# Softmax memory attention with two expert layers: clamps of the first weight conversions on GpSimd, first memory-times-weight products emitted earlier

## The chip, the cores and the metric

The kernel runs on one core of a Trainium2 chip. The time is that of one execution on the device, in microseconds (us). The engines are TensorE (PE; its weight loads are PEld), VectorE (DVE), ScalarE (ACT), GpSimd (POOL) and SyncE (SP), whose queue issues all DMAs. Each engine works through its instructions in the order in which the program gives them.

## The reference

For each of 8 x 8 heads (576 tokens, width 64, 32 memory slots):

```python
a = exp(phi - max(phi, tokens));  a = a / (sum(a, tokens) + 1e-9)
k_m = einsum('bhsm,bhsd->bhmd', a, k);  v_m = einsum('bhsm,bhsd->bhmd', a, v)
scores = q @ k_m.T / 8
attn = softmax(scores, memory slots)          # the kernel's p
x = attn @ v_m                                # [4608 tokens, 512]
```

Then two layers on the 4608 x 512 tokens, each with weights 512 x 2048 and 2048 x 512: `h = x @ w_in; x = (h - tanh(h)) @ w_out`, then `h = x @ w_in; out = elu(h) @ w_out`. The weights arrive as float64.

## The kernel before

Matrix products in the layers are done on pairs of a high and a low part (`hi`, `lo = a - hi`). In layer 1 the kernel does not form `attn @ v_m` first: it multiplies `v_m` with `w_in` (the `vw` products, lines 317 to 347), and then `vw` with p (`h_unit`, line 357, tile `h_ps`).

**Conversions.** `convert` (lines 40 to 64) turns 512 columns of float64 words into float32 with integer operations: the absolute value of the high word on ScalarE (line 48), a clamp of it on VectorE (line 50), a shift with a mask (line 51), and two more VectorE operations that add sign and low bits (lines 54, 57). The intermediate `cv_m` lies in PSUM, in a pool of one buffer. For the first four pages of `w_in` the last operation writes the weight itself (`whole`); otherwise it writes `cv_a` in SBUF (two buffers), ScalarE rounds it to `hi` (line 62) and GpSimd takes `lo` (line 64). A page is two conversions. The first 16 conversions are pages 0 to 3 of layer 1's `w_in` and `w_out`.

**Attention units.** The heads are worked off in 16 units of four heads (`unit`, from line 113). A unit reduces phi (`cmax`, line 123), transposes the maxima, spreads them with a matmul (`bmax`, line 136), subtracts (`a`, line 142), takes exponentials, forms k_m and v_m (`km`, line 157), transposes q (`pq`, line 182), forms scores (`sc`, line 202), transposes them on VectorE (line 204), and does the softmax: maximum and subtraction (lines 207, 208), exponential (line 210, ScalarE), sum, reciprocal and product (lines 212 to 215), transpose (line 218), `hi` and `lo` of p (lines 222, 223). Units 0 and 1 run these on VectorE; in later units `eng` is GpSimd for the operations written with `eng`. Units 0 and 1 send their p by DMA into the first blocks' tiles (line 230) as well as to DRAM (line 231). The phi tile has one buffer: the next unit's phi is loaded when `a` has been formed.

**The order of work.** The program's order is written by generators that are stepped in rounds: each `yield` ends a unit's or a conversion's step, `units.round()` and `cv.round()` step all that are alive. The prologue steps both until unit 1 is written out, and the two first `vw` pages come after that. Then 64 blocks of two `h_unit` calls follow, with conversions and units stepped between them; in block 1 a loop steps conversions and units together until the pages that it needs are converted. The set `converted` says that a conversion's instructions have been written into the program.

```python
        while 1 not in p_done:
            ...
            units.round()
            ...
        for pg in range(2):
            need("i", pg)
            m1.vw_whole(vm[0], wi[pg], pg, 0, 0)
```

Of the kernel before, what the change touches and what calls it, by code (L numbers as in the profile page):

```python
# [8 lines left out]
F32 = mybir.dt.float32  # L9
F32R = mybir.dt.float32r  # L10
I32 = mybir.dt.int32
U32 = mybir.dt.uint32
ACTF = mybir.ActivationFunctionType
ALU = mybir.AluOpType
# [4 lines left out]
B, H, S, D, M = 8, 8, 576, 64, 32  # L19
# [16 lines left out]
def r32(ap):  # L36
    return ap.bitcast(F32)


def convert(nc, pool, psum, raw, dst, whole=False):  # L40

    words = raw.bitcast(U32)
    w_lo, w_hi = words[:, 0::2], words[:, 1::2]
    lo_lim = 2.0 ** -15
    hi_lim = float.fromhex("0x1.fffffep+16")
    m = psum.tile(list(w_hi.shape), F32, tag="c", name="cv_m")
    mu = m.bitcast(U32)
    nc.scalar.activation(m, w_hi.bitcast(F32), ACTF.Abs)
    yield
    nc.vector.tensor_scalar(m, m, hi_lim, lo_lim, op0=ALU.min, op1=ALU.max)  # L50
    nc.vector.tensor_scalar(mu, mu, 3, 0x3FFFFFFF, op0=ALU.logical_shift_left, op1=ALU.bitwise_and)
    yield
    a = pool.tile(list(w_hi.shape), F32, tag="a", name="cv_a")
    nc.vector.scalar_tensor_tensor(mu, w_hi, 0xC0000000, mu, op0=ALU.bitwise_and, op1=ALU.bitwise_or)
    if whole:
        a = dst()
    nc.vector.scalar_tensor_tensor(a.bitcast(U32), w_lo, 29, mu, op0=ALU.logical_shift_right, op1=ALU.bitwise_or)
    if whole:
        return
    yield  # L60
    hi, lo = dst()
    nc.scalar.activation(hi, a, ACTF.Copy)
    yield
    nc.gpsimd.tensor_tensor(lo, a, r32(hi), op=ALU.subtract)  # L64


class Attention:
# [44 lines left out]
    def unit(self, u, nxt, eng, first_p=None):  # L112

        nc, wk, sm = self.nc, self.wk, self.sm
        b, g = divmod(u, 2)
        ident = self.ident
        kv, a, kT = self.kv, self.a, self.kT
# [5 lines left out]
        nc.vector.tensor_reduce(cmax, ph.rearrange("p h c m -> p h m c"), axis=AX.X, op=ALU.max)  # L123
        yield
        spaced = u >= 2
        mT = ps_tile([128, 96], "mT")
        nc.tensor.transpose(mT, cmax.rearrange("p h m -> p (h m)"), ident[:96, :96])
        nmax = sm.tile([128, 1], F32, tag="nmax", name="nmax")
# [8 lines left out]
        if spaced:  # L137
# [5 lines left out]
                          op=ALU.subtract)  # L143
# [31 lines left out]
        s = self.sc_p.tile([128, 18, M], F32, tag="s", name="s")  # L175
        for pr in range(2):
# [11 lines left out]
            if pr == 0:  # L188
# [6 lines left out]
                dst = self.vm_dst(b, g)  # L195
# [9 lines left out]
            yield  # L205
        smax = sm.tile([128, 18, 1], F32, tag="smax", name="smax")
        nc.vector.tensor_reduce(smax, s, axis=AX.X, op=ALU.max)
        nc.vector.tensor_tensor(s, s, smax.to_broadcast([128, 18, M]), op=ALU.subtract)
        yield
        nc.scalar.activation(s, s, ACTF.Exp, scale=1.0 / D ** 0.5)  # L210
        yield
        nc.vector.tensor_reduce(smax, s, axis=AX.X, op=ALU.add)
        nc.vector.tensor_scalar(smax, smax, GUARD, None, op0=ALU.add)
        nc.vector.reciprocal(smax, smax)
        eng.tensor_tensor(s, s, smax.to_broadcast([128, 18, M]), op=ALU.mult)
        yield
        pT = wk.tile([128, S], F32, tag="pT", name="pT")
        nc.vector.transpose(pT, s.rearrange("p j m -> p (j m)"))
# [1 line left out]
        phl = wk.tile([128, 2, 2, NB], F32R, tag="phl", name="phl")  # L220
        pTv = pT.rearrange("p (r s) -> p r s", r=2)
        nc.scalar.activation(phl[:, :, 0], pTv, ACTF.Copy)
        eng.tensor_tensor(phl[:, :, 1], pTv, r32(phl[:, :, 0]), op=ALU.subtract)
        yield
        if spaced:
            yield
# [304 lines left out]
def moe_kernel(tc, q, k, v, phi, w1, w2, w3, w4, out):  # L531
    nc = tc.nc
    with ExitStack() as top, tc.manual_schedule():
# [11 lines left out]
        m1 = Moe1(tc, l1a, const, p_dram, x2_dram)  # L545
# [3 lines left out]
        cv_p = new(l1b, "cv", 2, side="right")  # L549
# [3 lines left out]
        cv_ps = new(top, "ps_c", 1, space=PSUM)  # L553

        vm, vms = {}, {}
# [8 lines left out]
        wi, wo = {}, {}  # L564
        part = lambda t, h, c: t[:, h].rearrange("p a f -> p (a f)")[:, 512 * c:512 * c + 512]
        converted = set()

        def need(kind, pg, with_units=False):
            while not all((1, kind, pg, c) in converted for c in range(2)):
                cv.round()  # L570
                if with_units:
                    units.round()

        def conv(layer, kind, pg, c, lead=2):

            w = {("i", 1): w1, ("o", 1): w2, ("i", 2): w3, ("o", 2): w4}[kind, layer]
            raw = raw_p.tile([128, 512], mybir.dt.int64, tag="raw", name="raw")
            if kind == "i":
                src = w.rearrange("(k p) f -> p k f", p=128)[:, 2 * c:2 * c + 2, 256 * pg:256 * pg + 256]
                nc.sync.dma_start(out=raw.rearrange("p (a f) -> p a f", a=2), in_=src)  # L580
            else:
                r0 = 256 * pg + 128 * c
                nc.sync.dma_start(out=raw, in_=w[r0:r0 + 128, :])
            for k in range(lead + 1):
                yield k == lead
            staged, whole = [], (layer, kind) == (1, "i") and pg < 4

            def dst():
                if layer == 1:
                    ws = wi if kind == "i" else wo  # L590
                    if c == 0:
                        pool = wt_p[pg // 2 % (2 if kind == "i" else NSW)]
                        shape = [128, 2, 4, 256] if kind == "i" else [128, 2, 2, 512]
                        ws[pg] = pool.tile(shape, F32 if whole else F32R, tag=f"w{kind}{pg % 2}", name="w1")
                    if whole:
                        return part(ws[pg], 0, c)
                    return part(ws[pg], 0, c), part(ws[pg], 1, c)
                staged.append(wst_p[0].tile([128, 2, 512], F32R, tag="wst", name="wst"))
                return staged[-1][:, 0], staged[-1][:, 1]

            yield from convert(nc, cv_p, cv_ps, raw, dst, whole)
            converted.add((layer, kind, pg, c))
            if layer == 2:
                yield
                nc.sync.dma_start(out=w_dram[kind][pg, :, :, 512 * c:512 * c + 512], in_=r32(staged[-1]))

        conv_pair = lambda layer, kind, pg: [conv(layer, kind, pg, c) for c in range(2)]
        conv_l1 = lambda kind, *pgs: [g for pg in pgs for g in conv_pair(1, kind, pg)]
        conv_l2 = [g for pg in range(NPG) for kind in "io" for g in conv_pair(2, kind, pg)]
# [8 lines left out]
        for what in "phi", "kv", "q0", "q1":  # L618
            at0.load(0, what)
            at1.load(1, what)  # L620
        cv_first = [conv(1, "i", k // 2, k % 2, 0) for k in range(3)]
        cv = Staged([conv(1, "i", 1, 1)] + conv_l1("o", 0, 1), 2)
        cv.wait = 5
        for k, g in enumerate(cv_first):
# [3 lines left out]
        def unit(u):  # L628
            if u == 0:
                yield from at0.unit(u, 2 * B, nc.vector, first_p)  # L630
            else:
                yield from at1.unit(u, u + 1, nc.vector if u < 2 else nc.gpsimd, first_p if u == 1 else None)
# [2 lines left out]
        units = Staged()  # L635
        for u in range(2 * B):
            units.at((0, 1, 7, 13, 19, 25, 32, 39, 45, 52, 58, 65, 78, 85, 92, 99)[u], unit(u))
        while 1 not in p_done:
            if units.rounds >= 7:
                cv.half()  # L640
            units.round()
            if units.rounds >= 7:
                cv.round()
        pro.close()
        m1.ps_h = new(ps_h_ctx, "ps_h", 2, space=PSUM)
        at1.ps = misc
# [10 lines left out]
            nc.scalar.activation(vms[bp][:, 0], vm[bp], ACTF.Copy)  # L657
            nc.gpsimd.tensor_tensor(vms[bp][:, 1], vm[bp], r32(vms[bp][:, 0]), op=ALU.subtract)

        for pg in range(2):  # L660
            need("i", pg)
            m1.vw_whole(vm[0], wi[pg], pg, 0, 0)

# [6 lines left out]
        xq, pend, late = deque(), [], []  # L670
# [94 lines left out]
        for bi, (ss, bp, sub, j) in enumerate(blocks):  # L765
# [48 lines left out]
            for i in range(2):  # L814
                pg = 2 * sw + i
# [107 lines left out]
```

## Time and profile before

| what | us |
|---|---|
| median of 3 runs (1705.76 to 1710.95) | 1709.38 |
| the profiled execution, its own time | 1713.89 |
| its span, first to last instruction | 1712.1 |
| TensorE busy in the span | 1613.9 |
| first product of p with `vw` (`h_ps`, line 357) starts | 65.55 |

A row of a timeline gives the start and the duration of an instruction, or of several that follow each other, and in brackets the idle time of its engine ahead of it and what ended that. A row of waits sums the idle time of an engine ahead of a line by what ended it. TensorE's clock has two levels in the records, 1.2 and 2.4 GHz, given as 0.5 and 1.0.

### The profile page before, as it was taken

What the parts mean: (1) busy time and instruction counts of PE and PEld (TensorE: products, weight loads), DVE (VectorE), ACT (ScalarE), POOL (GpSimd) and SP (SyncE); (2) the same over time, 40 slices, a digit from 0 to 9 for tenths busy, and PEclk for the clock granted to TensorE, in tenths of its full rate; (3) what the DMA queues carried; (4) which work ended last, traced back from release to release, by engine and by line L of the source; (5) the groups of instructions that cost most, each with busy time, mean ns of one, the idle gap of its engine ahead of it and who ended that gap; (6) DMA issues with size and microseconds to landing.
All of it is one profiled execution on the core that took longest, in us unless ns stands there. A gap on an engine that the chain in (4) does not pass through costs nothing.

```text
span 1712.1 us, 26572 instructions
## 1 busy us (share of the span) xinstructions
PE 1613.9 (94%) x9884; PEld 1394.7 (81%) x9884; DVE 1187.0 (69%) x1730; ACT 931.0 (54%) x1677; POOL 757.2 (44%) x540
## 2 busy tenths in 40 slices
PE   5578999999989999999989999999999999999998
PEld 3346888787888999999989988888888888888886
DVE  4776767677989999999865655556555655565654
ACT  2455767677778888889853333333333333333332
POOL 1145655566666776767742222222222222222222
PEclk8668999999999999999999999999999999999999
DMA  8756566566565556666579321212121212121000
GB/s 194 213 172 179 176 188 198 182 201 226 192 212 176 170 193 219 220 214 215 182 238 360 103 62 48 74 49 63 49 74 42 70 50 74 50 65 59 25 14 25
DMA packets 140921, 236.09 MB, mean 138 GB/s; under 512 B 8184, under 2 KB 102392, under 8 KB 138744
## 3 DMA queue, kind: packets, MB, share of 16 engines
q1 hardware_dynamic: 140792, 234.39, 42.9%
q8 instruction: 78, 1.28, 0.3%
q14 instruction: 51, 0.42, 0.1%
HBM read 158.73 MB, written 74.45 MB: 136 GB/s over the span
## 4 chain that ended last, share of the span: by engine, by line
PE 65%; DVE 4%; DMA 4%; ACT 2%; issue 2%; POOL 1%; DVEq 0%; ACTq 0%; SPq 0%; POOLq 0%
PE h_ps L466 23%; PE o_ps L508 23%; PE x_ps L405 11%; PE h_ps L357 6%; PE vw_ps L328 1%; DMA p<-p_dram 1%; DMA xr<-x_dram 1%; DMA x_dram<-x 1%; DMA raw<-in_moe_w_in_dram 1%; DVE s L385 1%; DVE vw L333 1%; DVE h_ps L384 1%; ACT t L368 0%; DVE s L386 0%; POOL g L393 0%
## 5 line engine op out<-in xcount | busy, mean ns | idle before, releaser
L405 PE MATMUL x_ps<-g,w 128*128 128x288 f32 x3072 | 442.5, 297 | 11.8 <-POOL w L64 4.7
L492 POOL TENSOR_TENSOR e<-hm,e 128x512 fp32r<-128x512 f32 x144 | 187.1, 1299 | 576.9 <-ACT e L491 529.2
L405 PEld LDWEIGHTS x_ps<-g,w 128*128 128x128 f32 x3072 | 418.6, 189 | 25.6 <-ACT x L412 6.5
L466 PE MATMUL h_ps<-x,wi 128*128 128x512 f32 (+1 forms) x1920 | 424.6, 371 | 0.0
L508 PE MATMUL o_ps<-wo,e 128*128 128x512 f32 x1728 | 422.8, 393 | 0.7 <-POOL e L492 0.7
L466 PEld LDWEIGHTS h_ps<-x,wi 128*128 128x128 f32 x1920 | 336.1, 188 | 68.0
L508 PEld LDWEIGHTS o_ps<-wo,e 128*128 128x128 f32 x1728 | 323.4, 188 | 75.3 <-POOL e L492 1.1
L477 ACT ACTIVATE t_ps<-hm 128x512 f32<-128x512 f32 x144 | 86.7, 602 | 505.7 <-DVE hm L476 505.7
L375 POOL TENSOR_TENSOR v<-t,u 128x576 f32<-128x576 f32 x128 | 183.6, 1434 | 177.9 <-ACT u L369 161.1
L357 PE MATMUL h_ps<-p,vw 128*128 128x288 f32 x1536 | 240.2, 307 | 12.6 <-DVE s L386 6.6
L357 PEld LDWEIGHTS h_ps<-p,vw 128*128 128x128 f32 x1536 | 219.2, 196 | 24.5 <-issue 20.5
L483 DVE SCALAR_TENSOR_TENSOR hm<-hm,t_ps 128x512 f32<-128x512 f32 x144 | 99.1, 688 | 200.3 <-ACT hm L478 200.3
L393 POOL TENSOR_TENSOR g<-s,g 128x576 fp32r<-128x576 f32 x128 | 199.0, 1555 | 78.8 <-ACT g L392 71.5
L476 DVE TENSOR_SCALAR hm<-h_ps 128x512 f32<-128x512 f32 x144 | 99.6, 692 | 129.9 <-PE h_ps L466 129.2
L385 DVE SCALAR_TENSOR_TENSOR s<-s,v 128x576 f32<-128x576 f32 x128 | 137.3, 1073 | 7.3 <-POOL v L375 7.2
L368 ACT ACTIVATE t<-h_ps 128x576 f32<-128x576 f32 x128 | 83.3, 651 | 91.1 <-PE h_ps L357 38.8
L386 DVE COPY_PREDICATED s<-big,h_ps 128x576 f32<-128x576 uint32 x128 | 106.6, 833 | 12.8 <-ACT x L412 0.5
L370 ACT ACTIVATE s<-u,bias 128x576 f32<-128x576 f32 x128 | 99.5, 778 | 25.1 <-POOL g L393 15.5
L484 DVE SCALAR_TENSOR_TENSOR hm<-hm,t_ps 128x512 f32<-128x512 f32 x144 | 99.0, 688 | 5.0
L485 DVE TENSOR_TENSOR hm<-hm,h_ps 128x512 f32<-128x512 f32 x144 | 98.9, 687 | 5.0
L384 DVE TENSOR_TENSOR h_ps<-h_ps,t 128x576 f32<-128x576 f32 x128 | 96.6, 755 | 2.8 <-ACT u L369 2.7
L478 ACT ACTIVATE hm<-hm 128x512 f32<-128x512 f32 x144 | 91.0, 632 | 13.1
(88 smaller groups left out, 1681.2 us busy)
## 6 DMA issues: line engine op xcount, KB each, us to landing
x_dram<-x SPq DMA_DIRECT2D x128, 288.0 KB
xr<-x_dram SPq DMA_DIRECT2D x72, 512.0 KB
p<-p_dram SPq DMA_DIRECT2D x62, 576.0 KB
raw<-in_moe_w_in_dram SPq DMA_DIRECT2D x32, 512.0 KB
raw<-in_moe_w_out_dram SPq DMA_DIRECT2D x32, 512.0 KB
w_dram<-wst SPq DMA_DIRECT2D x32, 512.0 KB
kv<-in_k_dram SPq DMA_DIRECT2D x16, 576.0 KB
kv<-in_v_dram SPq DMA_DIRECT2D x16, 576.0 KB
```

What stands on the lines that cost most here:

```text
L357: nc.tensor.matmul(ps[:, j, :NB], lhsT=vw[a][:, kc, 128 * j:128 * j + 128], rhs=p[:, kc, b, :], start=(k == 0), stop=(k == 5))
L370: nc.scalar.activation(s, u, ACTF.Square, bias=bias[:, 0:1], scale=G_S)
L375: nc.gpsimd.tensor_tensor(v, t, u, op=ALU.mult)
L384: nc.vector.tensor_tensor(d, d, t, op=ALU.subtract)
L385: nc.vector.scalar_tensor_tensor(s, s, G_B, v, op0=ALU.add, op1=ALU.mult)
L386: nc.vector.copy_predicated(s, big.bitcast(U32), d)
L393: nc.gpsimd.tensor_tensor(g[:, 1], s, r32(g[:, 0]), op=ALU.subtract)
L405: nc.tensor.matmul(ps, lhsT=wo[pg][:, a, j, 128 * dm:128 * dm + 128], rhs=g[:, b, j, :], start=(k == 0), stop=(k == 11))
L466: nc.tensor.matmul(out, lhsT=w3[:, a, kc, 128 * j:128 * j + 128], rhs=x[:, b, kc, :], start=(i == 0), stop=(i == 11))
L476: nc.vector.tensor_scalar(hm, w[0], 0.0, None, op0=ALU.min)
L492: nc.gpsimd.tensor_tensor(e[:, 1], hm, r32(e[:, 0]), op=ALU.subtract)
L508: nc.tensor.matmul(acc, lhsT=e[:, a, jj, 128 * tg:128 * tg + 128], rhs=w4[:, b, j, :], start=(k == 0 and jj == 0 and i == 0), stop=(k == l ...
```

## The change

For the first 16 conversions ScalarE writes the absolute value to `cv_a` in SBUF, GpSimd clamps it there, and VectorE's first operation is the shift, from SBUF to `cv_m`. Both are written in the step of the absolute value, so a conversion has one step less. In unit 0 the subtraction of the maximum, the product with the reciprocal and the `lo` of p go to GpSimd (`beside`, `late`). The two first `vw` pages are written in the prologue, each as soon as its two conversions and `v_m` of units 0 and 1 are written.

```diff
-def convert(nc, pool, psum, raw, dst, whole=False):
+def convert(nc, pool, psum, raw, dst, whole=False, apart=False):
...
+    if apart:
+        a = pool.tile(list(w_hi.shape), F32, tag="a", name="cv_a")
+        nc.scalar.activation(a, w_hi.bitcast(F32), ACTF.Abs)
+        nc.gpsimd.tensor_scalar(a, a, hi_lim, lo_lim, op0=ALU.min, op1=ALU.max)
+        yield
+        m = psum.tile(list(w_hi.shape), F32, tag="c", name="cv_m")
+        mu = m.bitcast(U32)
+        nc.vector.tensor_scalar(mu, a.bitcast(U32), 3, 0x3FFFFFFF, op0=ALU.logical_shift_left, op1=ALU.bitwise_and)
+    else:
...
         spaced = u >= 2
+        beside = nc.gpsimd if u == 0 else nc.vector
+        late = eng if spaced else beside
...
-        nc.vector.tensor_tensor(s, s, smax.to_broadcast([128, 18, M]), op=ALU.subtract)
+        beside.tensor_tensor(s, s, smax.to_broadcast([128, 18, M]), op=ALU.subtract)
...
-        eng.tensor_tensor(s, s, smax.to_broadcast([128, 18, M]), op=ALU.mult)
+        late.tensor_tensor(s, s, smax.to_broadcast([128, 18, M]), op=ALU.mult)
...
-        eng.tensor_tensor(phl[:, :, 1], pTv, r32(phl[:, :, 0]), op=ALU.subtract)
+        late.tensor_tensor(phl[:, :, 1], pTv, r32(phl[:, :, 0]), op=ALU.subtract)
...
-            yield from convert(nc, cv_p, cv_ps, raw, dst, whole)
+            yield from convert(nc, cv_p, cv_ps, raw, dst, whole, layer == 1 and pg < 4)
...
+        vw_now = deque(range(2))
         while 1 not in p_done:
...
+            if vw_now and {0, 1} <= vm_done and all((1, "i", vw_now[0], c) in converted for c in range(2)):
+                pg = vw_now.popleft()
+                m1.vw_whole(vm[0], wi[pg], pg, 0, 0)
...
-        for pg in range(2):
+        for pg in vw_now:
             need("i", pg)
             m1.vw_whole(vm[0], wi[pg], pg, 0, 0)
```

The line numbers of the changed kernel are higher: its clamp is line 49, its shift 53, lines 54 and 57 are 63 and 66, line 123 is 132, 136 is 147, 157 is 168, 182 is 193, 202 is 213, 204 is 215, 207 to 223 are 218 to 234, 344 and 347 are 355 and 358.

TensorE's queue in the opening, before, from unit 2's transposed maxima to unit 2's `km`:

```order
L127 MATMUL mT<-ident,cmax 128x96
L182 MATMUL pq<-ident,q 128x96 x3
L202 MATMUL sc<-qT,kT 64x288 x2
L182 MATMUL pq<-ident,q 128x96 x6
L136 MATMUL bmax<-dmax,ones 96x128
L202 MATMUL sc<-qT,kT 64x288 x2
L182 MATMUL pq<-ident,q 128x96 x3
L202 MATMUL sc<-qT,kT 64x288 x2
L157 MATMUL km<-kv,a 32x192 x24
```

The same stretch in the changed kernel:

```order
L138 MATMUL mT<-ident,cmax 128x96
L193 MATMUL pq<-ident,q 128x96 x3
L213 MATMUL sc<-qT,kT 64x288 x2
L355 MATMUL vw_ps<-w_334,vm 64x256 x4
L193 MATMUL pq<-ident,q 128x96 x6
L147 MATMUL bmax<-dmax,ones 96x128
L213 MATMUL sc<-qT,kT 64x288 x2
L193 MATMUL pq<-ident,q 128x96 x3
L213 MATMUL sc<-qT,kT 64x288 x2
L355 MATMUL vw_ps<-w_413,vm 64x256 x4
L168 MATMUL km<-kv,a 32x192 x24
```

The two `vw` pages now stand ahead of the second q transposes of units 0 and 1, and ahead of unit 2's `km`.

VectorE's queue, before, from the last scores of unit 1 to the transpose of unit 0's softmax (`w_415` is page 1 of `w_in`):

```order
L57 SCALAR_TENSOR_TENSOR w_415<-raw,cv_m 128x512
L207 TENSOR_REDUCE smax<-s 128x18
L208 TENSOR_TENSOR s<-s,smax 128x576
L123 TENSOR_REDUCE cmax<-phi 96x128
L50 TENSOR_SCALAR cv_m<-cv_m 128x512
L51 TENSOR_SCALAR cv_m<-cv_m 128x512
L212 TENSOR_REDUCE smax<-s 128x18
L213 TENSOR_SCALAR smax<-smax 128x18
L214 RECIPROCAL smax<-smax 128x18
L215 TENSOR_TENSOR s<-s,smax 128x576
```

The same stretch in the changed kernel:

```order
L218 TENSOR_REDUCE smax<-s 128x18
L219 TENSOR_TENSOR s<-s,smax 128x576
L132 TENSOR_REDUCE cmax<-phi 96x128
L53 TENSOR_SCALAR cv_m<-cv_a 128x512
L63 SCALAR_TENSOR_TENSOR cv_m<-raw,cv_m 128x512
L66 SCALAR_TENSOR_TENSOR w_413<-raw,cv_m 128x512
L358 TENSOR_TENSOR vw<-vw_ps,vw 128x512
L223 TENSOR_REDUCE smax<-s 128x18
L224 TENSOR_SCALAR smax<-smax 128x18
L225 RECIPROCAL smax<-smax 128x18
```

All of page 1's second conversion and the `lo` of its `vw` product now stand ahead of unit 0's sum (line 212, now 223), and the product that followed (line 215) has left the queue.

GpSimd's queue of the opening in the changed kernel, where before the two `a` of units 2 and 3 stood alone:

```order
L49 TENSOR_SCALAR cv_a<-cv_a 128x512 x3
L153 TENSOR_TENSOR a<-phi,bm 96x4x6x32
L219 TENSOR_TENSOR s<-s,smax 128x576
L49 TENSOR_SCALAR cv_a<-cv_a 128x512
L226 TENSOR_TENSOR s<-s,smax 128x576
L49 TENSOR_SCALAR cv_a<-cv_a 128x512
L234 TENSOR_TENSOR phl<-pT,phl 128x2x288
L49 TENSOR_SCALAR cv_a<-cv_a 128x512
L153 TENSOR_TENSOR a<-phi,bm 96x4x6x32
```

Of the 16 clamps, five belong to conversions whose VectorE part stands ahead of unit 1's `lo` of p (line 223, now 234); eleven come later. Further on, from block 1 to the last unit, each unit stands one step later against the blocks than before: before, seven `h_unit` calls are ahead of the eleventh pair of scores (line 202), now eight.

## Rows read from the trace of the kernel before

**Rows 1.** The page, part 1: busy time and share of the span by engine.
```profile
PE 1613.9 (94%) x9884; PEld 1394.7 (81%) x9884; DVE 1187.0 (69%) x1730; ACT 931.0 (54%) x1677; POOL 757.2 (44%) x540
```

**Rows 2.** Windows: us, busy us (x instructions) of each engine, clock, DMA.
```profile
30.50:62.10 31.60, 17.33 (x102) 8.92 (x102) 28.93 (x52) 8.91 (x19) 2.11 (x2) 0.58 0.62 163
300.00:350.00 50.00, 47.01 (x376) 40.47 (x376) 32.80 (x47) 35.73 (x72) 28.73 (x22) 1.00 0.56 176
400.00:450.00 50.00, 48.79 (x390) 43.03 (x389) 43.17 (x64) 38.32 (x77) 34.95 (x24) 1.00 0.60 210
```

**Rows 3.** Waits of 0 to 120 us: waiter <- releaser, us, times, longest.
```profile
DVE cmax L123 <- DMA phi<-in_phi_dram: 10.9, 3, 6.2
PE vw_ps L344 <- DVE w L57: 2.9, 1, 2.9
```

**Rows 4.** Timeline of the opening, VectorE: start us, us, instruction.
```profile
30.52 1.44 DVE L123 TENSOR_REDUCE cmax<-phi 96x128 f32<-96x768 f32 x1 [6.19 <-DMA phi<-in_phi_dram]
38.05 0.69 DVE L57 SCALAR_TENSOR_TENSOR w<-raw,cv_m 128x512 uint32<-128x512 uint32 x1
41.55 0.84 DVE L208 TENSOR_TENSOR s<-s,smax 128x576 f32<-128x576 f32 x1
48.20 0.74 DVE L212 TENSOR_REDUCE smax<-s 128x18 f32<-128x576 f32 x1
49.49 0.76 DVE L215 TENSOR_TENSOR s<-s,smax 128x576 f32<-128x576 f32 x1
51.32 0.69 DVE L57 SCALAR_TENSOR_TENSOR w<-raw,cv_m 128x512 uint32<-128x512 uint32 x1
57.23 0.75 DVE L223 TENSOR_TENSOR phl<-pT,phl 128x576 fp32r<-128x576 f32 x1
61.29 0.76 DVE L223 TENSOR_TENSOR phl<-pT,phl 128x576 fp32r<-128x576 f32 x1 [1.31 <-ACT phl L222]
```

**Rows 5.** Timeline of the opening, TensorE.
```profile
34.07 1.22 PE L182 MATMUL pq<-ident,q 96*128 96x96 f32 x6
46.14 4.01 PE L157 MATMUL km<-kv,a 96*32 96x192 f32 x48 [5.14 <-ACT a L148]
57.68 3.18 PE L344 MATMUL vw_ps<-w,vm 128*64 128x256 f32 x16
65.55 3.22 PE L357 MATMUL h_ps<-p,vw 128*128 128x288 f32 x12 [4.69 <-DMA p<-phl]
```

**Rows 6.** Timeline of the opening, GpSimd and the DMA queue of SyncE.
```profile
39.97 1.80 POOL L142 TENSOR_TENSOR a<-phi,bm 96x768 f32<-96x768 f32 x1 [36.75 <-ACT bm L140]
41.80 0.31 SPq L106 DMA_DIRECT2D phi<-in_phi_dram  x1
62.08 2.43 SPq L230 DMA_DIRECT2D p<-phl  x4
```

**Rows 7.** Lines of GpSimd, whole span: xcount, busy us, mean ns.
```profile
L64 POOL TENSOR_TENSOR w<-cv_a,w 128x512 fp32r<-128x512 f32 x24 | 31.5, 1313 | 1.1 <-ACT w L62 1.1
L215 POOL TENSOR_TENSOR s<-s,smax 128x576 f32<-128x576 f32 x14 | 16.8, 1199 | 26.6 <-DVE smax L214 22.2 <-ACT big L379 4.0 <-ACT u L369 0.4
L133 POOL TENSOR_SCALAR dmax<-ident,nmax 128x128 f32<-128x128 f32 x10 | 7.2, 717 | 0.0
```

**Rows 8.** Lines of VectorE, 30 to 62 us.
```profile
L50 DVE TENSOR_SCALAR cv_m<-cv_m 128x512 f32<-128x512 f32 x6 | 4.2, 693 | 0.4 <-ACT cv_m L48 0.3
```

**Rows 9.** Timeline: one VectorE operation alone, then beside GpSimd.
```profile
35.47 0.24 DVE L133 TENSOR_SCALAR dmax<-ident,nmax 128x128 f32<-128x128 f32 x1
81.85 1.40 POOL L375 TENSOR_TENSOR v<-t,u 128x576 f32<-128x576 f32 x1 [7.97 <-ACT u L369]
81.88 1.46 DVE L133 TENSOR_SCALAR dmax<-ident,nmax 128x128 f32<-128x128 f32 x1
```

**Rows 10.** Waits of TensorE from 165 to 600 us.
```profile
PE km L157 <- ACT a L148: 3.0, 3, 2.0
PE sc L202 <- ACT kT L194: 1.1, 2, 0.9
```

More of the change, by code (lines that the diff above doesn't have):

```diff
@@ L45, in convert @@
     hi_lim = float.fromhex("0x1.fffffep+16")
[L46 to L53, printed above, removed]
+    if apart:
[7 more added lines that the diff above has]
+    else:
+        m = psum.tile(list(w_hi.shape), F32, tag="c", name="cv_m")
+        mu = m.bitcast(U32)
+        nc.scalar.activation(m, w_hi.bitcast(F32), ACTF.Abs)
+        yield
+        nc.vector.tensor_scalar(m, m, hi_lim, lo_lim, op0=ALU.min, op1=ALU.max)
+        nc.vector.tensor_scalar(mu, mu, 3, 0x3FFFFFFF, op0=ALU.logical_shift_left, op1=ALU.bitwise_and)
+        yield
+        a = pool.tile(list(w_hi.shape), F32, tag="a", name="cv_a")
     nc.vector.scalar_tensor_tensor(mu, w_hi, 0xC0000000, mu, op0=ALU.bitwise_and, op1=ALU.bitwise_or)
```

## The prediction

> **What bounds the kernel now.** I read the page first. TensorE is busy for 94% of the span [rows 1], so over the whole program the work on TensorE sets the time, and what a change can win or lose are the stretches in which TensorE stands still or starts late. The widest of them is the opening: the first product of p with `vw` starts at 65.55 us, and it had waited for the DMA that brings unit 1's p [rows 5]. What comes before it is therefore worth its full length, as long as nothing else is late.
>
> Next I read the windows. From 30.5 to 62.1 us VectorE is busy for 28.93 of 31.60 us, GpSimd for 2.11 and TensorE for 17.33, the latter at a mean granted clock of 0.58, so mostly at the lower of its two levels, 1.2 GHz [rows 2]. In that stretch VectorE is the bound: p of unit 1 leaves behind VectorE's `lo` at 61.29, and the DMAs are issued at 62.08 [rows 4, 6]. Before it VectorE stands 6.2 us for unit 2's phi, until 30.52 [rows 3, 4].
>
> **The change part by part.** The clamps: VectorE loses five of them, of 0.69 us each, ahead of unit 1's `lo` [rows 8], and unit 0's three operations, of 0.84, 0.76 and 0.75 us [rows 4]. That is 3.45 + 2.35 = 5.8 us of work taken from the bounding engine. GpSimd has the room. Were the queues otherwise unchanged, the first block would start up to 5.8 us earlier.
>
> They are not unchanged, and I follow the two `vw` pages through them. "When its parts are there" is judged while the program is written; on the chip the instruction simply stands in its queue and waits.
>
> Page 0. TensorE is done with what stands ahead of it at 34.07, where the six q transposes began before [rows 5]. VectorE cannot begin before phi at 30.52. Before, the second conversion's last operation ended at 38.05 + 0.69 = 38.74 [rows 4]; two clamps less give 37.4. Both pages together took TensorE 3.18 us [rows 5]; the half of one page that needs the second conversion is a quarter of that, 0.8. So the q transposes start at 38.2 instead of 34.07: 4.1 us later, and `bmax`, the scores and the rest of the queue with them.
>
> What follows from that is another engine's wait. ScalarE's copy of `bmax` and GpSimd's `a` of unit 2 (39.97 before, 1.80 long) come later, and phi of unit 3 is issued only behind `a` (41.80) [rows 6]. Of the 4.1 us I let 3 reach `a`: an absolute value no longer waits for VectorE to free `cv_m`, so ScalarE comes a little sooner to its copies (an estimate). VectorE's `cmax` of unit 3 needs that phi and stands ahead of page 1's second conversion, whose end, 51.32 + 0.69 = 52.0 before [rows 4], I put at 51.7: 3 us later for phi, about as much earlier for four clamps and unit 0's subtraction.
>
> Page 1. TensorE reaches it at about 44 and stands until 51.7, then needs 0.8 us: `km` of unit 2, at 46.14 before [rows 5], starts at 52.5, 6.4 us late. The `lo` of this page stands on VectorE ahead of unit 0's sum. It waits for TensorE, and for ScalarE's copy (0.6, an estimate from VectorE's 0.69 on the same 128x512 shape [rows 8]), and lasts 0.7: the sum starts at about 54.1 instead of 48.20 [rows 4]. That is 5.9 us late.
>
> From there to unit 1's `lo` it was 61.29 - 48.20 = 13.1 us. Taken out of this stretch are unit 0's product and `lo` (0.76 + 0.75), one clamp (0.69) and the two operations of conversion 3 that now stand ahead of it (1.4): 3.6. Put in are the way to GpSimd and back for the product, 1.20 instead of 0.76 [rows 4, 7] with two hand-overs, 0.6 in all; unit 1's product, which can stand for up to 1.0 behind GpSimd's `lo` of unit 0; and ScalarE's rounding of conversion 4 ahead of unit 1's (0.6): 2.2. So unit 1's `lo` starts at 61.29 + 5.9 - 3.6 + 2.2 = 65.8, and **the first block is 4.5 us late**. I keep 3 to 7 as its bounds.
>
> After the first block. Eleven conversions are left. Their clamps were at most 11 x 0.69 = 7.6 us on VectorE's path, at least nothing. TensorE waited for a conversion's last operation for 2.9 us in all up to 120 us [rows 3]; I take that, **-2.9**. A clamp on GpSimd has no row. The nearest are a 128x128 operation with a scalar operand, 0.72, and a 128x512 operation with two tensors, 1.31 [rows 7]; shape and place speak for the second, the single tensor for the first, and I take 1.0. The Trainium skill, GPSIMD Engine Reference, section Engine selection, calls GpSimd roughly line-rate for one input, which would put it near the lower row and take about 0.6 us off the next term; no run here shows it yet. Eleven clamps are 11 us of new work in GpSimd's queue, ahead of `a` and of the blocks' products; nothing of it need show (GpSimd was mostly idle), all of it can. I take two of them, in front of an `a` that is waited for: **+2**.
>
> The later units. Each stands one step later against the blocks, with the same work. TensorE's two waits that belong to units, between 165 and 600 us, are 3.0 for `a` and 1.1 for kT [rows 10]: 4.1 us, which could go or double. The units' ends now lie a step deeper in the stretch where the second layer's conversions run and VectorE is busy for 43.17 of 50 us, against 32.80 a hundred us earlier [rows 2]. So I take the side of the loss: **+3**, of bounds -4.1 and +4.1.
>
> The sum: +4.5 - 2.9 + 2 + 3 = **+6.6 us**. The profiled execution took 1713.89 (its span 1712.1), so it would be 1720.5; it lay 4.5 us above the median of the runs, 1709.38, and against that the forecast is **1716.0 us**, 0.4% slower.
>
> **The rivals.** First, the relief wins (faster). The 5.8 us come off VectorE and TensorE's waits for the pages are covered: then -5.8 - 2.9 + 2 = -6.7, 1702.7 us. For it speaks VectorE's 28.93 of 31.60 us. Against it speaks the first `vw` page's place: this case needs page 0's second conversion written by 34.07, that is phi of unit 2 some 3.3 us sooner, and for page 1 still more. It decides at VectorE's idle time ahead of `cmax`.
>
> Second, the delay is made good (same). The first block is 4.5 us late, but all eleven clamps were on the path and GpSimd's cost nothing: +4.5 - 7.6 = -3.1, 1706.3 us; with the units' +3 it is no change at all. For it: conversions and units keep VectorE busier than GpSimd in all the windows [rows 2]. Against: after the first block the waits of TensorE that end in a conversion are few [rows 3].
>
> Third, GpSimd and VectorE hold each other up (slower still). VectorE's 128x128 operation took 0.24 us alone and 1.46 when it began 0.03 us after a GpSimd operation of 1.40 [rows 9]: it waited until GpSimd was done. If each of the eleven later clamps holds such an operation for its 1.0 us, the loss is +4.5 - 2.9 + 11 + 3 = +15.6, 1725.0 us; with 1.31 per clamp it is 1728.4. Against: the row shows it for an operation that has SBUF operands alone, and each VectorE operation of a conversion writes PSUM or reads it; it takes a product of two SBUF tensors in a block or a unit, close behind a clamp. The Trainium skill, GPSIMD Engine Reference, section Specifications, names the SBUF interfaces shared with VectorE, with contention for its two-port modes and for two SBUF inputs; by that rule this rival would come true, and the row agrees for the one operation it shows.
>
> That the change does nothing is excluded by the queues shown above.
>
> **How the numbers follow.** Chances: the forecast 0.45, the third rival 0.18, the second 0.24, the first 0.13. A measurement of this kernel tells about 0.3%, 5.1 us, from no change; faster is the first rival, 0.13, same the second, 0.24, slower the forecast and the third, 0.63. The low end takes in the second rival and part of the first: 1704.5, which is the forecast with every clamp as relief and the units' waits gone (4.5 - 7.6 + 2 - 4.1 = -5.2). The high end is the third rival with a late first block of 7 and a clamp of 1.2: 7 - 2.9 + 13.2 + 3 = +20.3, 1729.7.
>
> **What would show it.** In the changed profile: TensorE idle ahead of both `vw` pages, released by the conversions' last VectorE operation, about 3 us at the first and over 6 at the second; VectorE idle ahead of the `lo` of `vw`, released by ScalarE; unit 2's `km` near 52 and the first `h_ps` near 70. A first `h_ps` before 65 would refute the walk. A clamp of more than 1.3 us, or VectorE products of two SBUF tensors longer by a microsecond between 70 and 170 us, would be the third rival. If the first `h_ps` is late and the tenth is not, it is the second.

## The result and the profile after

The changed kernel takes **1735.00 us** (median of 4 runs, 1730.94 to 1736.13), the kernel before 1708.93 beside it: ratio 1.0141, 95% interval 1.0124 to 1.0158. It is slower, as forecast, but by 26.1 us of the medians (24.1 by the ratio, 1.41% of 1709) instead of 6.6, and outside the range. The profiled execution took 1736.13, its span 1734.3; before it was 1713.89.

The page's first part, after, in answer to [rows 1]:

```profile
PE 1620.2 (93%) x9884; PEld 1399.3 (81%) x9884; DVE 1177.7 (68%) x1711; ACT 930.3 (54%) x1677; POOL 771.4 (44%) x559
```

VectorE lost 19 instructions and GpSimd has 19 more. TensorE has as many as before and is busy 6.3 us longer; the other 15.9 of the 22.2 us by which the span grew are TensorE standing still. The windows of [rows 2], after (window, its length, busy us of PE, PEld, DVE, ACT, POOL, then clock, DMA share, GB/s):

```profile
30.50:62.10 31.60, 17.47 (x97) 8.43 (x98) 22.24 (x41) 7.65 (x15) 7.31 (x7) 0.95 0.44 122
300.00:350.00 50.00, 48.46 (x389) 41.83 (x388) 36.94 (x56) 35.62 (x69) 28.90 (x21) 1.00 0.64 199
400.00:450.00 50.00, 40.65 (x302) 34.13 (x303) 33.15 (x53) 28.45 (x58) 21.02 (x16) 0.86 0.59 190
```

VectorE's relief in the opening is there (22.24 for 28.93 us), and so is GpSimd's room. The surprise is the last row: TensorE is busy 8 us less than before between 400 and 450, and its mean clock falls to 0.86, where it had the higher of its two levels, 2.4 GHz, throughout. No clamp runs there; the last of the 16 starts at 151.7.

The opening went as the prediction walked it. TensorE after, in answer to [rows 5] (start, duration, instruction, in brackets the idle time ahead and what ended it):

```profile
36.13 1.94 PE L355 MATMUL vw_ps<-w,vm 128*64 128x256 f32 x6 [2.06 <-DVE w L66]
38.00 1.22 PE L193 MATMUL pq<-ident,q 96*128 96x96 f32 x6
...
50.80 1.97 PE L355 MATMUL vw_ps<-w,vm 128*64 128x256 f32 x6 [6.17 <-DVE w L66]
52.70 3.44 PE L168 MATMUL km<-kv,a 96*32 96x192 f32 x48
...
71.12 3.22 PE L368 MATMUL h_ps<-p,vw 128*128 128x288 f32 x12 [7.78 <-DMA p<-phl]
```

VectorE after, in answer to [rows 4]:

```profile
29.32 1.46 DVE L132 TENSOR_REDUCE cmax<-phi 96x128 f32<-96x768 f32 x1 [4.66 <-DMA phi<-in_phi_dram]
...
50.06 0.69 DVE L66 SCALAR_TENSOR_TENSOR w<-raw,cv_m 128x512 uint32<-128x512 uint32 x1
53.44 0.69 DVE L358 TENSOR_TENSOR vw<-vw_ps,vw 128x512 fp32r<-128x512 f32 x1 [2.69 <-ACT vw L357]
54.05 0.74 DVE L223 TENSOR_REDUCE smax<-s 128x18 f32<-128x576 f32 x1
...
58.60 1.63 DVE L226 TENSOR_TENSOR s<-s,smax 128x576 f32<-128x576 f32 x1
...
65.45 0.76 DVE L234 TENSOR_TENSOR phl<-pT,phl 128x576 fp32r<-128x576 f32 x1 [1.13 <-ACT phl L233]
```

Both `vw` pages stand in TensorE's queue until the conversion's last operation, 2.06 and 6.17 us; the first `h_ps` starts at 71.12, 5.6 us later than before.

Where the other 18 us came from is seen by numbering the `h_ps` products (12 instructions each) and taking the start of each minus its start before. These are worked out from the timelines of four profiled executions. That of before was 4.5 to 5 us slower than its median and that of `fewer` 2.5 us faster, so the last row is smaller for `fewer` than the difference of the medians further down:

| product | before, us | after | fewer | steps |
|---|---|---|---|---|
| 0 | 65.6 | +5.6 | -0.9 | -1.9 |
| 18 | 237.7 | +2.3 | -6.6 | -2.9 |
| 20 | 252.9 | +7.9 | -0.8 | -2.9 |
| 36 | 367.2 | +8.2 | -0.5 | -2.6 |
| 38 | 383.9 | +3.6 | -5.1 | -0.7 |
| 40 | 402.5 | +15.8 | +8.4 | +0.4 |
| 46 | 439.7 | +23.3 | +12.1 | +0.5 |
| 127 | 888.6 | +22.1 | +12.7 | +1.9 |

(`fewer` and `steps` are experiments below.) At products 18 and 38 after and `fewer` gain for a moment, by order alone: before, a unit's `km` stands ahead of that product, in after behind it. Counted from product 36, after loses 15.1 us up to product 46, the largest loss. The timeline of after shows the larger place; first VectorE and TensorE:

```profile
394.00 0.69 DVE L66 SCALAR_TENSOR_TENSOR cv_a<-raw,cv_m 128x512 uint32<-128x512 uint32 x1
402.54 1.44 DVE L132 TENSOR_REDUCE cmax<-phi 96x128 f32<-96x768 f32 x1 [7.85 <-DMA phi<-in_phi_dram]
403.91 0.68 DVE L358 TENSOR_TENSOR vw<-vw_ps,vw 128x512 fp32r<-128x512 f32 x1
...
394.54 1.86 PE L416 MATMUL x_ps<-g,w 128*128 128x288 f32 x12 [0.26 <-ACT qT L195]
404.64 1.23 PE L213 MATMUL sc<-qT,kT 128*64 128x288 f32 x4 [8.24 <-DVE vw L358]
```

VectorE stands 7.85 us for the phi of unit 15. Behind that `cmax` in its queue stands the `lo` of a `vw` page, and TensorE waits 8.24 us for it. The same stretch in SyncE's queue and on GpSimd:

```profile
353.43 0.31 SPq L118 DMA_DIRECT2D q<-in_q_dram  x1
361.74 0.31 SPq L115 DMA_DIRECT2D phi<-in_phi_dram  x1
...
388.39 0.33 SPq L115 DMA_DIRECT2D phi<-in_phi_dram  x1
...
359.87 1.85 POOL L153 TENSOR_TENSOR a<-phi,bm 96x768 f32<-96x768 f32 x1 [1.33 <-ACT bm L151]
```

The load of unit 15's phi is issued at 388.39, 6.3 us ahead of where VectorE is ready for it (394.7), and `cmax` starts 14.1 us behind the issue. Before, the same unit:

```profile
367.19 0.51 SPq L109 DMA_DIRECT2D q<-in_q_dram  x1
376.49 0.33 SPq L106 DMA_DIRECT2D phi<-in_phi_dram  x1
...
380.14 0.80 DVE L386 COPY_PREDICATED s<-big,h_ps 128x576 f32<-128x576 uint32 x1
380.83 1.52 DVE L123 TENSOR_REDUCE cmax<-phi 96x128 f32<-96x768 f32 x1
```

Issue at 376.49, `cmax` at 380.83 without a wait. phi had 4.3 us and was there. So the lead of the load over its use did not shrink (4.3 us before, 6.3 after); its landing came later.

### The profile page after: what moved, and what is told of

Its sections match the earlier page's. It is cut to its first block, busy times and chain, and to the rows that moved or that the text cites. A ratio compares the mean times of both kernels' runs of the same rounds, so it can differ in the third digit from the quotient of the medians.

```text
span 1734.3 us, 26585 instructions
## 1 busy us (share of the span) xinstructions
PE 1620.2 (93%) x9884; PEld 1399.3 (81%) x9884; DVE 1177.7 (68%) x1711; ACT 930.3 (54%) x1677; POOL 771.4 (44%) x559
## 4 chain that ended last, share of the span: by engine, by line
PE 66%; DMA 2%; DVE 2%; issue 1%; ACT 1%; POOL 0%; DVEq 0%; ACTq 0%; SPq 0%; POOLq 0%
PE h_ps L477 23%; PE o_ps L519 23%; PE x_ps L416 12%; PE h_ps L368 6%; PE vw_ps L339 1%; DMA xr<-x_dram 1%; DMA raw<-in_moe_w_in_dram 1%; DVE s L396 1%; DMA p<-p_dram 1%; DVE vw L344 1%; DVE h_ps L395 0%; PE vw_ps L355 0%; ACT t L379 0%; DMA p_dram<-phl 0%; DVE s L397 0%
## 5 line engine op out<-in xcount | busy, mean ns | idle before, releaser
L416 PE MATMUL x_ps<-g,w 128*128 128x288 f32 x3072 | 446.2, 299 | 12.1 <-POOL w L73 5.1
L390 ACT ACTIVATE big<-u,bias 128x576 f32<-128x576 f32 x128 | 98.0, 766 | 2.1 <-DVE s L397 2.1
```

Source lines behind the costliest of these rows:

```text
L416: nc.tensor.matmul(ps, lhsT=wo[pg][:, a, j, 128 * dm:128 * dm + 128], rhs=g[:, b, j, :], start=(k == 0), stop=(k == 11))
```

## The experiments

Theory 1: the conversions' lost step moved the units against the blocks, and that shift is the large part. Theory 2: the clamps load GpSimd and hold VectorE. Theory 3: the early `vw` pages cost all of it. The difference below is (ratio - 1) x 1709 us.

| run | median us | ratio to before (95%) | difference |
|---|---|---|---|
| after | 1735.00 | 1.0141 (1.0124 to 1.0158) | +24.1 |
| steps | 1712.93 | 1.0015 (0.9999 to 1.0031) | +2.6 |
| fewer | 1729.15 | 1.0118 (1.0101 to 1.0135) | +20.2 |
| novw | 1727.49 | 1.0100 (1.0084 to 1.0117) | +17.1 |
| onlyvw | 1717.24 | 1.0046 (1.0031 to 1.0061) | +7.9 |
| steps_novw | 1707.17 | 0.9979 (0.9965 to 0.9993) | -3.6 |
| steps_clamp | 1709.35 | 0.9988 (0.9974 to 1.0003) | -2.1 |
| clamp3 | 1713.31 | 1.0014 (1.0004 to 1.0023) | +2.4 |
| phi2 | 1717.51 | 1.0041 (1.0025 to 1.0058) | +7.0 |
| phi2_late | 1723.46 | 1.0078 (1.0050 to 1.0105) | +13.3 |
| phiq | 1733.36 | 1.0138 (1.0123 to 1.0153) | +23.6 |
| phi2_before | 1709.69 | 0.9995 (0.9976 to 1.0013) | -0.9 |
| phi2_novw | 1711.64 | 1.0003 (0.9992 to 1.0014) | +0.5 |
| phi2_sn | 1709.94 | 0.9988 (0.9972 to 1.0005) | -2.1 |
| open_vw | 1710.89 | 1.0002 (0.9992 to 1.0013) | +0.3 |
| open_novw | 1709.41 | 0.9994 (0.9982 to 1.0007) | -1.0 |
| open2_vw | 1709.11 | 0.9989 (0.9977 to 1.0001) | -1.9 |
| open2_novw | 1708.73 | 0.9995 (0.9983 to 1.0008) | -0.9 |

### The shift, undone and alone

`steps`, on the changed kernel:

```diff
         nc.vector.tensor_scalar(mu, a.bitcast(U32), 3, 0x3FFFFFFF, ...)
+        yield
     else:
```

> The changed kernel with one more yield in the conversions whose clamp is on GpSimd (behind the shift), so that they have as many steps as before and every later unit stands against the blocks where it stood before. Clamps, unit 0's operations on GpSimd and the early vw pages stay. Theory 1 (the step that each conversion lost shifted the units, and the shift costs about 18 of the 26 us): 1709 + 6 to 9 = 1715 to 1718 us, first h_ps still at 70 to 71 us, no single wait of 8 us between 380 and 410 us. Theory 2 (the clamps load GpSimd and hold VectorE): unchanged, 1730 to 1736. Theory 3 (the early vw pages cost all of it, the shift nothing): unchanged, 1730 to 1736.

`fewer`, on the kernel before, for the first 16 conversions:

```diff
-    yield
+    if not apart:
+        yield
     a = pool.tile(list(w_hi.shape), F32, tag="a", name="cv_a")
```

> The kernel before with one yield less in its first 16 conversions (the clamp stays on VectorE, no early vw page, unit 0 on VectorE): the shift of the units alone. Theory 1: 1709 + 12 to 20 = 1721 to 1729 us, with the loss after 350 us. Theories 2 and 3: 1706 to 1712, as before.

The extra `yield` takes 21.5 of the 24.1 us away, with clamps, early pages and unit 0 on GpSimd left in. But it does more than undo the shift: the pages are written later too, page 1 behind unit 2's `km` instead of ahead of it, and the first `h_ps` starts at 63.6, where theory 1 expected 70 to 71; the time lies 2 us below its range. `fewer` is the clean test. One `yield` less in each of the first 16 conversions of the kernel before, and nothing else, costs 20.2 us, at the upper end of theory 1's range. Theories 2 and 3 had said "unchanged" for both. `fewer` shows the same place as after, though its opening is not late at all:

```profile
394.30 1.44 DVE L124 TENSOR_REDUCE cmax<-phi 96x128 f32<-96x768 f32 x1 [8.31 <-DMA phi<-in_phi_dram]
...
396.40 1.23 PE L203 MATMUL sc<-qT,kT 128*64 128x288 f32 x4 [8.71 <-DVE vw L348]
```

### The early pages, taken away and alone

`novw` (changed kernel) and `onlyvw` (`apart` never set and `beside` always VectorE):

```diff
-            if vw_now and {0, 1} <= vm_done and ...
+            if False and vw_now and {0, 1} <= vm_done and ...
```

> The changed kernel without the early vw pages (both stand behind the prologue, as before). Theory 1: the shift stays, the late first block goes: first h_ps at 61 to 65 us, 1722 to 1729 us. Theory 2: 1730 to 1736. Theory 3: 1706 to 1710.

> The kernel before with the two early vw pages alone (conversions with all their steps and the clamp on VectorE, unit 0 on VectorE). Theory 1: only the late first block, 1709 + 4 to 9 = 1713 to 1718 us, first h_ps at 71 to 75 us (no clamp and no operation of unit 0 is taken from VectorE). Theory 2: 1709 to 1713. Theory 3: 1730 to 1736.

Both times are theory 1's. The first `h_ps` was at 60.1 in `novw`, a little sooner than expected, and at 72.1 in `onlyvw`. The early pages cost 7.0 us there and 7.9 here. With the shift's 20.2 and the clamps' -3.6 (next) the parts add to 24.5, against 24.1 measured.

### The clamps

`steps_novw` is `steps` without the early pages; `steps_clamp` also has `beside = nc.vector`; `clamp3` writes the clamp of `steps_novw` three times.

> The changed kernel with the extra yield and without the early vw pages: clamps and unit 0's three operations on GpSimd alone, units and blocks standing to each other as before. Theory 1, by adding the runs so far (1712.9 for the extra yield, less 1735.0 - 1727.5 = 7.5 for the early pages): 1705.4 us; range 1702 to 1708. If the clamps' relief and the early pages do not add: 1708 to 1712.

> The kernel of steps_novw with unit 0's three operations back on VectorE: the sixteen clamps on GpSimd alone, all steps as before. If unit 0's operations were part of the gain: 1708 to 1711 us, first h_ps 1 to 2 us later than in steps_novw (59.6). If the clamps made all of it: 1705 to 1708.

> The kernel of steps_novw with each of the sixteen clamps written three times (the result is the same): 32 more operations of 0.63 us, 20 us more on GpSimd. Theory 1 (GpSimd has the room, a clamp costs next to nothing): 1707 + 0 to 6 = 1707 to 1713 us. Theory 2 (a clamp holds VectorE or the queue behind it for its length): 1707 + 15 to 25 = 1722 to 1732 us.

Clamps and unit 0's three operations on GpSimd win 3.6 us (interval 1.2 to 6.0), the only version whose interval lies below 1. The clamps alone give 2.1, unclear against nothing and against 3.6. Thirty-two more clamps cost 6.0 us (2.4 + 3.6), 0.19 us each, just above theory 1's range (1713.31 against 1713) and far from theory 2's. Their rows, lines of GpSimd in `clamp3` (count, busy us, mean ns, idle time ahead):

```profile
L49 POOL TENSOR_SCALAR cv_a<-cv_a 128x512 f32<-128x512 f32 x16 | 11.0, 685 | 40.4 <-ACT cv_a L48 40.3
L51 POOL TENSOR_SCALAR cv_a<-cv_a 128x512 f32<-128x512 f32 x16 | 10.6, 662 | 1.3
L50 POOL TENSOR_SCALAR cv_a<-cv_a 128x512 f32<-128x512 f32 x16 | 10.4, 650 | 1.3
```

### Is it phi?

`phi2`: two buffers for phi, and from unit 2 on the next unit's load at a unit's start instead of behind `a`; the number of steps stays.

```diff
-            t = self.wk.tile([96, 4, 6, M], F32, tag="phi", name="phi")
+            t = self.phi_p.tile([96, 4, 6, M], F32, tag="phi", name="phi")
...
         nc.vector.tensor_reduce(cmax, ...)
+        if eng is nc.gpsimd:
+            self.load(nxt, "phi")
...
         if eng is nc.gpsimd:
-            self.load(nxt, "phi")
             yield
```

> The changed kernel with two buffers for phi: from unit 2 on, the next unit's phi is loaded at a unit's start instead of behind its a, some 15 us sooner. The shift of the units stays. Theory 1a (the shift costs what it costs because the phi of units 10 and 15 lands late: VectorE stands 2.6 and 7.9 us at cmax, TensorE 2.5 and 8.2 behind it, then a lower clock): 1735 - 10 to 17 = 1718 to 1725 us. Theory 1b (phi is where it shows, but another wait takes its place, of the units' ends with the blocks' p): 1730 to 1735 us.

> The kernel before with the same two buffers for phi. After 60 us VectorE waits for phi 6.6 us in three places there, none above 3.0, and TensorE 1.4 behind it. Theory 1a: a gain of 0 to 4 us, 1705 to 1710. Theory 1b: 1707 to 1712.

17.1 of the 24.1 us are gone with the shift in place, and the same buffers do nothing measurable for the kernel before. So most of what the shift costs hangs on how early phi is loaded. In `phi2` unit 15's load is issued 32.9 us ahead of its `cmax`, and VectorE does not wait (SyncE's queue, then VectorE):

```profile
357.53 0.32 SPq L116 DMA_DIRECT2D phi<-in_phi_dram  x1
...
390.42 1.60 DVE L133 TENSOR_REDUCE cmax<-phi 96x128 f32<-96x768 f32 x1
```

What is left, 7.0 us, is what the early pages cost (7.9 alone), less the clamps' 3.6, and 2.7 us that stay unexplained; the profiled execution of `phi2` was the slowest of its ten runs (1725.84), so its late part is not used for that. Without the early pages, and with the buffers on top of `steps_novw`:

> The changed kernel with two buffers for phi and without the early vw pages. By adding the runs so far, 1735.0 - 17.5 (two buffers) - 7.5 (early pages): 1710 us, range 1705 to 1713. If the steps that the conversions save are worth something once phi is in time (without the early pages the eighth h_ps came 12.7 us sooner than before): 1699 to 1705 us, faster than both kernels.

> The kernel of steps_novw with two buffers for phi. Theory 1a, by adding: 1705 less 0 to 4 = 1701 to 1706 us, faster than both kernels. Theory 1b: as steps_novw.

`phi2_novw` came out where adding put it (+0.5), so the saved steps are worth nothing. `phi2_sn` (-2.1) did not beat `steps_novw`: theory 1a had expected a gain, and theory 1b's "as `steps_novw`" is what came.

These two and the pair before them make a square without the early pages. The shift costs 20.7 us with one buffer (`novw` less `steps_novw`) and 2.6 with two (`phi2_novw` less `phi2_sn`), about the 2.7 left over above and not clear of noise. Not all of the loss at the largest place is phi's wait, though: from product 36 to 46 `phi2_novw` still loses 5.8 us against before, after 15.1. What makes that rest is not shown.

### Why phi is late

In after, SyncE's queue stands from 353.74 to 361.74 for GpSimd's `a`, which ends at 361.72; from 355 to 362 us the DMA engines are nearly idle:

```profile
355.00:362.00 7.00, 6.32 (x46) 5.48 (x45) 4.45 (x8) 4.67 (x11) 3.71 (x4) 1.00 0.07 25
```

The reading to be tested is that what was held back then bunches ahead of the next phi. `phiq` issues phi from unit 3 on by GpSimd instead; `phi2_late` is `phi2` with the load at its old place.

```diff
-            nc.sync.dma_start(out=t, in_=view("phi", 0, 4))
+            (nc.gpsimd if u > 2 else nc.sync).dma_start(out=t, in_=view("phi", 0, 4))
```

> The changed kernel with one buffer for phi, whose loads from unit 3 on are issued from GpSimd's queue right behind a instead of from SyncE's. Theory 1c (what makes phi late is SyncE's queue: it stands behind phi's load until a is formed, 8.0 us from 353.7 to 361.7 us, so that the blocks' p, x, kv and weights bunch ahead of the next phi): SyncE no longer stands there, phi of unit 15 lands within 8 us, 1718 to 1725 us, as with two buffers. Theory 1d (phi is late because it is asked for only behind a, at a time when the DMA engines are three quarters busy anyway): phi of unit 15 still lands 10 us or more behind its issue, 1728 to 1735 us.

> The changed kernel with two buffers for phi, but with phi's load at its old place in SyncE's queue, behind where a is written. The load then no longer waits for a, and SyncE does not stand there. Theory 1c (SyncE's standing behind phi makes the transfers bunch and phi late): 1716 to 1722 us, as with the load at the unit's start (1717.5). Theory 1d (phi is asked for too late, whoever waits for it): phi of unit 15 still holds VectorE for 5 us or more, 1726 to 1735 us.

Neither settled it. In `phiq` phi of unit 15 did land within 6.3 us, as theory 1c said, but the time is theory 1d's: in other units VectorE now waited for phi (4.0 us at units 8 and 11, 3.5 at unit 14); at units 11 and 14 between `a` and the load 1.4 to 2.5 us of other products stood in GpSimd's queue. Issue and use in `phiq`:

```profile
393.05 0.73 POOL L115 DMA_DIRECT2D phi<-in_phi_dram  x1
...
399.38 1.59 DVE L132 TENSOR_REDUCE cmax<-phi 96x128 f32<-96x768 f32 x1
```

The Trainium skill, DMA: Bandwidth & Descriptors, section Issuing engines are not separate DMA queues, says that DMAs of all engines run on the same DMA engines and that a second issuer saves only issue time. `phiq`'s total (+23.6) agrees in so far as nothing was won, but its later issue in other units can make that too, so no run here shows it.

`phi2_late`, at +13.3, lies below theory 1d's range and above 1c's. Its SyncE does not stand, yet phi still needs 13.2 us; it is only asked for further ahead:

```profile
373.59 0.60 SPq L116 DMA_DIRECT2D phi<-in_phi_dram  x1
...
386.81 1.52 DVE L133 TENSOR_REDUCE cmax<-phi 96x128 f32<-96x768 f32 x1 [1.14 <-DMA phi<-in_phi_dram]
```

A longer lead covers the late landing at unit 15: 6.3 us in after, 12.1 here with 1.1 of wait left, 32.9 in `phi2`. That the queue's standing alone makes phi late does not fit the kernel before: there it stands as long, from 367.70 to 376.49, but unit 15's phi is the first load behind it (DMA share 0.49 from 369 to 376), where in after the DMA engines are 0.76 busy from 382 to 388, just ahead of the issue. Why the transfer took 13 to 14 us where it took at most 4.3 before, through which of the transfers beside it, stays open.

### Why the early pages cost

The first rival had named a condition: phi of unit 2 some 3.3 us sooner. `open_vw` and `open_novw` (two buffers, all steps, with and without the early pages) moved that load to unit 1's start:

> The changed kernel with the extra yield (units and blocks as before), two buffers for phi, and phi of unit 2 loaded at unit 1's start instead of behind its exponential. The early vw pages stay. If the early pages cost because unit 2's phi comes late (VectorE stood 4 to 6 us for it): first h_ps 2 to 5 us sooner than with the extra yield alone (63.7), 1712.9 less 2 to 5 = 1708 to 1711 us. If they cost because of their place in TensorE's queue whatever phi does: 1711 to 1715.

> The same without the early vw pages. If VectorE's wait for unit 2's phi is on the path of the first block: first h_ps 2 to 5 us sooner than in steps_novw (59.6), 1707.2 less 2 to 5 = 1702 to 1705 us, faster than both kernels. If the other loads of the opening, which now stand behind it, take its place: 1706 to 1711.

This edit missed. Three weight loads still stood ahead, the load was issued at 17.3 as before, and VectorE waited 4.4 and 5.5 us. `open2_vw` and `open2_novw` write it ahead of them:

```diff
+        at1.load(2, "phi")
         cv_first = [conv(1, "i", k // 2, k % 2, 0) for k in range(3)]
```

> As open_vw, but phi of unit 2 is loaded ahead of the first three weight loads, behind the opening's q. Early vw pages stay, units and blocks as before. If the early pages cost because unit 2's phi comes late: VectorE's wait for it (4.4 us) is gone, page 0's wait on TensorE falls below 1 us, first h_ps at 58 to 61 us, 1704 to 1708 us. If they cost because of their place in TensorE's queue, or the weights now come as much later: first h_ps at 62 to 66, 1709 to 1714.

> The same without the early vw pages. If VectorE's wait for unit 2's phi is on the path of the first block: first h_ps at 55 to 58 us, 1702 to 1706 us, faster than both kernels. If the weights now come as much later, or VectorE's work was not what ended last: 1706 to 1711.

Now the load is issued at 9.77, VectorE does not wait for it, and TensorE in `open2_vw` hardly waits for the pages:

```profile
33.05 0.83 PE L356 MATMUL vw_ps<-w,vm 128*64 128x256 f32 x5 [0.33 <-DVE w L67]
...
47.94 1.97 PE L356 MATMUL vw_ps<-w,vm 128*64 128x256 f32 x6 [0.63 <-DVE w L67]
...
62.58 3.22 PE L369 MATMUL h_ps<-p,vw 128*128 128x288 f32 x12 [4.70 <-DMA p<-phl]
```

But it is not phi that took these waits away. In `steps` phi is late and they are as short:

```profile
27.54 1.48 DVE L133 TENSOR_REDUCE cmax<-phi 96x128 f32<-96x768 f32 x1 [3.82 <-DMA phi<-in_phi_dram]
...
34.16 1.54 PE L356 MATMUL vw_ps<-w,vm 128*64 128x256 f32 x5 [0.21 <-DVE w L67]
42.87 4.07 PE L169 MATMUL km<-kv,a 96*32 96x192 f32 x48 [3.92 <-ACT a L160]
48.97 1.97 PE L356 MATMUL vw_ps<-w,vm 128*64 128x256 f32 x6 [0.63 <-DVE w L67]
63.63 3.22 PE L369 MATMUL h_ps<-p,vw 128*128 128x288 f32 x12 [4.72 <-DMA p<-phl]
```

They went with the pages' later place in TensorE's queue, which all versions with the extra `yield` share. Nor do these waits set the price: the pages cost 7.0 us in the changed kernel, where TensorE waits 8.2 us for them, 6.2 in `steps` (less `steps_novw`), where it waits 0.8, and 7.9 in `onlyvw`, where it waits 1.8.

With and without the early pages the `open2` times are 1709.11 and 1708.73: the pages cost nothing measurable. The same holds with phi late: `open_vw` less `open_novw` is 1.3 us by the ratios, with intervals that overlap. So the late phi of unit 2 is not shown to be why the pages cost, and `open2_vw` landed in the second range of its expectation, by time and by its first `h_ps` (62.6). The four `open` versions have two buffers for phi and load it at a unit's start, `steps` does not; why the pages' cost goes there stays open. They win nothing either: the first `h_ps` is still 2.2 us behind that of `open2_novw` (60.3). And `open2_novw` is no faster than `steps_novw`, so VectorE's wait for unit 2's phi was not on the path by itself.

## Why the prediction was right and wrong

- **The first block, +4.5: right for this kernel, in part by luck.** It was 5.6, inside 3 to 7. The q transposes were put at 38.2 and came at 38.00, `km` of unit 2 at 52.5 and 52.70, unit 0's sum at 54.1 and 54.05, unit 1's `lo` at 65.8 and 65.45. TensorE's two waits ended with the conversions' last operations, as the walk had it. The luck is in the parts: the conversions were done sooner than put (36.13 for 37.4, 50.80 for 51.7), and the rest of each page took longer, 1.94 and 1.97 us for 0.8, because six of its eight products stood behind the wait and not half of them. Unit 0's sum by the terms written down is 53.8, not 54.1. And the waits are not what the pages cost over the whole program: `onlyvw` and `steps` have little of them and lose about as much.
- **The clamps, -2.9 and +2: not refuted, not measured apart.** The two terms make -0.9. Clamps and unit 0's operations measure -3.6 together, of which the opening's part stood in the first term; no run takes the -2.9 by itself. For each extra clamp 0.19 us showed; +2 for eleven is 0.18. A clamp took 0.63 us in the mean, below the lower bound of 0.72:

```profile
L49 POOL TENSOR_SCALAR cv_a<-cv_a 128x512 f32<-128x512 f32 x16 | 10.1, 630 | 53.4 <-ACT cv_a L48 49.4 <-DVE pT L229 4.0
```

  VectorE needed 0.69 for the same shape [rows 8], so the Trainium skill, GPSIMD Engine Reference, section Engine selection, is borne out with its rough line rate for one input; taking 0.6 instead of 1.0 would have made no difference to the result.
- **The later units, +3 with bounds -4.1 and +4.1: wrong, and nearly the whole error of 17.5 us.** The step measured 20.2 us (`fewer`) and 20.7 (`novw` less `steps_novw`). It failed where the text said that the two waits of TensorE that belong to units "could go or double". That bounds a shift by the waits that exist [rows 10]. A wait that does not exist yet has no row there; phi of unit 15 arrived in time before with at most 4.3 us from issue to use. What the runs showed in its place is that load landing late: VectorE waits 7.85 us for it and TensorE 8.24 behind VectorE, and with phi loaded early the step costs 2.6. The waits for phi that the trace of after shows at units 10 and 15 (2.6 and 7.85 us) do not add to 20; how the rest follows from the shift is not shown. There was a warning that the prediction did not use: its rows of waits for phi ended at 120 us [rows 3]. Past that, VectorE before also waited for phi of units 9 and 14:

```profile
210.37 1.54 DVE L123 TENSOR_REDUCE cmax<-phi 96x128 f32<-96x768 f32 x1 [1.68 <-DMA phi<-in_phi_dram]
...
358.15 1.55 DVE L123 TENSOR_REDUCE cmax<-phi 96x128 f32<-96x768 f32 x1 [2.95 <-DMA phi<-in_phi_dram]
```

  Which units pay depends on how units and blocks stand to each other: in after it is no longer 9 and 14 but 10 (2.6 us) and 15. Why the landing of unit 15's phi came so late stays open.
- **First rival (relief wins): fell.** In the changed kernel the waits that stood against it were there. But where they are covered and the shift is undone, -6.7 does not come either: `steps` measured +2.6 and `open2_vw` -1.9.
- **Second rival (delay made good): fell.** The tenth `h_ps` was 2.5 us late, so a part was made good, and then lost again.
- **Third rival (GpSimd and VectorE hold each other up): there, but small.** VectorE's product of unit 1, 0.76 us before (as unit 0's in [rows 4]), took 1.63 at 58.60, beside this GpSimd operation:

```profile
58.22 1.40 POOL L234 TENSOR_TENSOR phl<-pT,phl 128x576 fp32r<-128x576 f32 x1 [1.03 <-ACT phl L233]
```

  Its sign showed in part: from 70 to 170 us the units' subtraction of the maximum took 1.39 us in the mean of three, 0.86 before. `clamp3` prices it: 0.19 us a clamp, not 1.0. The rule in the Trainium skill, GPSIMD Engine Reference, section Specifications, is seen at work on operations of two SBUF inputs, but would have given the wrong sum.
- **A slip in the range.** Its low end is added up as -5.2, which is 1704.2 and not 1704.5; it changes nothing here.

## What to carry to other kernels

Where code is stepped by generators, a `yield` is part of the schedule: taking one out of one stream moves every other stream against it, for the rest of the program, and that can cost far more than the work that was moved. When a change shifts streams, list for each transfer its lead over its use and how long it takes to land; a load that is used a few us behind its issue can turn into a wait, and a row of waits shows only those that are late already. Keep the number of steps when an operation changes its engine, or give such a load a second buffer first.

## What the runs showed of the hardware

- The same load of phi, 288 KB, was there at most 4.3 us after its issue before, and 14.1 us after it in the changed kernel. One late transfer of this size held TensorE for 8.24 us.
- In the opening, from 30.5 to 62.1 us, the mean granted clock reads 0.95 after and 0.58 before [rows 2], but TensorE's instructions show no faster clock after: six q transposes took 1.22 us in both (38.00 after, 34.07 before). Six products of a page took 1.94 us at 36.13, where at the higher level eight took 1.08 (393.20, below). The clock records in the trace of after begin at 55.4 us, and the mean counts the time ahead of them as full speed.

```profile
393.20 1.08 PE L355 MATMUL vw_ps<-w,vm 128*64 128x256 f32 x8
```

- While TensorE stood for 8.24 us the clock fell to the lower level, at 400.1 us, for 10.2 us: 0.86 in the mean from 400 to 450 us. Products 40 to 46 lost another 7.5 us there in after, but that is not shown to be the clock: in `phi2_novw`, without this wait and with a mean of 1.00 in the same window, they lost 6.0.
